# adaLN block on one core: K, Q and V's bias and the sum of phi(K) taken out of the products, through a column of ones, with smaller early loads and a new order

## The chip, the cores and the metric

The kernel runs on one core of one Trainium2 chip. The metric is the device time of one execution in microseconds (us). Engines are named as in the profile: PE (TensorE, matrix products; PEld is its weight load), DVE (VectorE), ACT (ScalarE), POOL (GpSimd) and SP (SyncE, which here only issues DMAs). PSUM is the memory into which PE writes its sums; SBUF is the working memory that all engines read.

## The reference

```python
mod = (silu(c) @ w_mod).reshape(1, 6, 1, 512)
sa, ca, ga, sb, cb, gb = (mod[:, i] for i in range(6))
h = layernorm(x) * (1 + ca) + sa                 # x: 1 x 2048 x 512
q, k, v = split(h @ wqkv)                        # 32 heads of 16
pq, pk = phi(q), phi(k)                          # phi(t) = where(t > 0, t + 1, exp(t)) + 1e-6
kv = einsum("bhsd,bhse->bhde", pk, v)
z  = einsum("bhsd->bhd", pk)
o  = einsum("bhqd,bhde->bhqe", pq, kv) / (einsum("bhqd,bhd->bhq", pq, z)[..., None] + 1e-6)
x  = x + ga * (o.reshape(1, 2048, 512) @ wo)
h  = layernorm(x) * (1 + cb) + sb
u  = gelu(h @ w_in)                              # 512 -> 1376, halves z1 and z2
g  = w_sp @ layernorm(z2) + b_sp                 # w_sp: 2048 x 2048, over the rows
x  = x + gb * ((z1 * g) @ w_out)
```

The attention is linear: with G = h^T phi(K) (512 x 512), the matrix kv follows from V's weights and G, so V itself is never formed.

## The kernel before, in words

The 2048 rows are 16 tiles of 128. Every product in full precision is made of three products of rounded halves (fp32r, "hi" and "lo"): `mm3` issues hi x hi, hi x lo and lo x hi, its lines 94, 95 and 96 in the profile. A tile's split is one copy on ACT (hi) and one subtraction on DVE or POOL (lo). A few small products are plain fp32.

Part A: load a tile of x, take mean and variance on DVE (`s1`, `ln_stats`; the power -0.5 runs on POOL), shift it (`s2`), split it (`s2_hi`, `s2_lo`: tile `hhl`), transpose it (`tx` on PE, `ht` after the split), and multiply it with K's and Q's weights (`kp`, `qp`, four chunks of 128 rows of the weights, three products of 512 columns each, so 12 products a tile). phi gives `pk` and `pq`; `g_mm` sums G over the tiles in two pairs of PSUM banks (`g0` and `g1`, alternating). From G come `gh` (its split), `kv_mm` and `kv_mask` (block diagonal), `m2_mm` (kv times wo, tile `pm`), then `den1`, `den2` and `wo_mm` (tile `po`). Part B is z (`win`), gelu, layernorm, the spatial product by seven products instead of eight (tile `P`, 2 x 2 blocks, f the sums of blocks), and the output product (tile `pn`).

Modulation: `pcol1` is the scale 1 + ca as a column of four chunks (PE products of w_mod with silu(c)), `pcol0` the shift sa. Before the change:

- `s2` makes X = mean - x, without the reciprocal deviation; `col_end` stores -(1 + ca), and `w_hi`, `w_lo` multiply K's, Q's and V's weights by it. The deviation comes later, as a scale of `phi_in` or `phi_raw`, and of `pk_hi` and `pk_lo`.
- The biases of K and Q (sa times the weights, `bias_part`, `bias_prod`, `bias_add`) are summed to rows, spread over all partitions by a product with ones (`bias_row`), kept as `kqb` and added on DVE (`phi_in`, `phi_add`).
- phi is `phi_in` or `phi_raw` from PSUM, then `phi_exp` (two ACT operations) and `phi_end` (DVE).
- V's bias is a column (`v_prod`, `v_add`, `col_v`, tile `pcolv`), which `v_bias` multiplies with z to `bz`; `kv_mask` adds it. z is the sum of phi(K) over the rows, collected tile by tile by `pk_sum`, split by `z_split` and summed over the partitions by `z_sum` (tile `pz`).

What runs when is written out by hand. A long string `ORDER` lists two-letter names of steps with their numbers (`OPS` maps them to functions; a step that is a generator goes on to its next yield at each mention). Each engine executes its instructions in the order in which the string issues them, so a waiting instruction holds up all that stand behind it on its engine. A second string, `SLOTS`, says which buffer of a pool the next tile takes: `psb` (pairs of PSUM banks), `pst` and `pso` (single banks; `pso` has two), the others in SBUF. All loads are issued by SP in the same order. `dummy` issues a product of ones with ones into a scratch tile (`warm`).

Of the kernel before, what the change touches and what calls it, by code (L numbers as in the profile page):

```python
# [37 lines left out]
u:0101100110101010
# [4 lines left out]
def block_kernel(ctx: ExitStack, tc: tile.TileContext, x, w_qkv, w_o, w_in, w_sp, b_sp, w_out,  # L43
# [64 lines left out]
    nc.gpsimd.memset(tiny, TINY)  # L108

# [19 lines left out]
    def load_w(j, h):  # L129
        load_raw(("qkv", j, h), w_qkv[j, :, 2 * h:2 * h + 2, :], parts=2 if (j, h) == (1, 0) else 1)  # L130

    def load_m(m, h):
        load_raw(("mod", m, h), w_mod[m, :, 2 * h:2 * h + 2, :], tag="zs", parts=2 if h else 1)
# [40 lines left out]
    def col_end(key):  # L174
        COL[key] = const.tile([P, KC], F32, name=f"col{key}")
        if key == 1:
            nc.scalar.activation(COL[key], CP[key][:, :, 0], AF.Copy, scale=-1.0, bias=-1.0)
# [37 lines left out]
    MEAN, RSTD = {}, {}  # L215

    def ln_stats(key, src, n):
# [10 lines left out]
        nc.gpsimd.tensor_tensor(mv[:, 1:2], ve, mhalf, op=OP.pow)  # L228

# [97 lines left out]

    def bias_row(j):
        p = ps("t", [P, D], f"bias{j}")
        for h in range(2):  # L330
            mm(p, ones, BY[j][:, h], start=h == 0, stop=h == 1)
        BY[j] = p

    def bias_end(j):
        if j == 1:
            kqb.append(sb("zs", [P, 2, D], F32, "kqb"))
        nc.scalar.activation(kqb[0][:, 1 - j], BY.pop(j), AF.Copy, bias=TINY)
# [48 lines left out]
    KP, QP, PK, PKHL, PQ, EK, TK = {}, {}, {}, {}, {}, {}, {}  # L386

    def k_mm(t, lo=0, hi=KC):
        if lo == 0:
            KP[t] = ps("o", [P, D], f"kp{t}")  # L390
        for kc in range(lo, hi):
            mm3(KP[t], HT[t][:, 0, kc], HT[t][:, 1, kc], w_of(1, kc)[:, 0], w_of(1, kc)[:, 1], kc == 0, kc == KC - 1)

    def q_mm(t):
        QP[t] = ps("o", [P, D], f"qp{t}")
        for kc in range(KC):
            mm3(QP[t], HT[t][:, 0, kc], HT[t][:, 1, kc], w_of(0, kc)[:, 0], w_of(0, kc)[:, 1], kc == 0, kc == KC - 1)
        HT.pop(t)


    def phi_in(key, p, b):
        TK[key] = sb("tb", [P, D], F32, f"t{key[0]}{key[1]}")
        nc.vector.scalar_tensor_tensor(TK[key], p, RSTD["a", key[1]], b, op0=OP.mult, op1=OP.add)


    def phi_raw(key, p):
        if key[0] == "q":
            if key[1] // 2 not in PQT:
                PQT[key[1] // 2] = sb("zs", [P, 2, D], F32, f"pq{key[1] // 2}")
            TK[key] = PQT[key[1] // 2][:, key[1] % 2, :]  # L410
        else:
            TK[key] = sb("zs", [P, D], F32, f"t{key[0]}{key[1]}")
        nc.scalar.activation(TK[key], p, AF.Copy, scale=RSTD["a", key[1]])

    def phi_add(key, b, e=0):
        ENG[e].tensor_add(TK[key], TK[key], b)

    def phi_exp(key):
        EK[key] = sb("tb", [P, D], F32, f"e{key[0]}{key[1]}")
        nc.scalar.activation(EK[key], TK[key], AF.Relu, scale=-1.0, bias=tiny)  # L420
        yield
        nc.scalar.activation(EK[key], EK[key], AF.Exp, scale=-1.0)
# [6 lines left out]
    def q_end(t):  # L429
# [820 lines left out]
```

## Time and profile before

| | us |
|---|---|
| median of 3 runs | 613.09 (611.5 to 613.3) |
| profiled execution, its own time | 614.38 |
| span of the profile | 612.6 |
| PE busy | 602.3 |
| DVE busy | 484.7 |
| ACT busy | 387.3 |
| POOL busy | 274.3 |

The span runs from the first to the last instruction; the time of an execution is the span and some 2 us around it. Busy times are sums over one engine's instructions. The mean granted clock of PE is 0.997 of full speed. In the rows of a timeline the first number is the start, the second the length, and the square brackets tell how long the engine had been idle and what ended that.

### The profile page before, as it was taken

What the parts mean: (1) busy time and instruction counts of PE and PEld (TensorE: products, weight loads), DVE (VectorE), ACT (ScalarE), POOL (GpSimd) and SP (SyncE); (2) the same over time, 40 slices, a digit from 0 to 9 for tenths busy, and PEclk for the clock granted to TensorE, in tenths of its full rate; (3) what the DMA queues carried; (4) which work ended last, traced back from release to release, by engine and by line L of the source; (5) the groups of instructions that cost most, each with busy time, mean ns of one, the idle gap of its engine ahead of it and who ended that gap; (6) DMA issues with size and microseconds to landing.
All of it is one profiled execution on the core that took longest, in us unless ns stands there. A gap on an engine that the chain in (4) does not pass through costs nothing.

```text
span 612.6 us, 9781 instructions
## 1 busy us (share of the span) xinstructions
PE 602.3 (98%) x3510; PEld 560.4 (91%) x3510; DVE 484.7 (79%) x840; ACT 387.3 (63%) x614; POOL 274.3 (45%) x249
## 2 busy tenths in 40 slices
PE   8999999999899999999999999999999999999997
PEld 8787888878788999999999999999999999998996
DVE  5889999996898976877768987755567677999874
ACT  4998999765657555955857745456464446484451
POOL 4132341414645434535652053465584524245874
PEclk9899999999999999999999999999999999999999
DMA  8555786441669564662522526275745758677673
GB/s 276 198 161 143 175 281 188 126 164 35 235 201 229 139 184 143 117 144 67 111 82 94 195 93 169 90 209 149 211 134 157 173 175 224 225 189 246 217 214 119
DMA packets 95792, 102.36 MB, mean 167 GB/s; under 512 B 65952, under 2 KB 66208, under 8 KB 95744
## 3 DMA queue, kind: packets, MB, share of 16 engines
q1 hardware_dynamic: 95744, 101.74, 57.6%
q8 instruction: 27, 0.44, 0.3%
q14 instruction: 21, 0.17, 0.1%
HBM read 61.09 MB, written 25.17 MB: 141 GB/s over the span
## 4 chain that ended last, share of the span: by engine, by line
PE 89%; DVE 4%; ACT 2%; DMA 2%; issue 1%; SPq 0%; DVEq 0%
PE P L890 34%; PE z L653 20%; PE po L96 2%; PE po L95 2%; PE pn L94 2%; PE po L94 2%; PE pn L95 2%; PE pn L96 2%; DMA raw_mod<-in_w_mod 2%; PE kp L94 2%; PE kp L96 2%; PE kp L95 2%; PE g L96 2%; PE g L94 2%; PE g L95 2%; PE qp L94 2%
## 5 line engine op out<-in xcount | busy, mean ns | idle before, releaser
L890 PE MATMUL P<-f,f 128*128 128x344 f32 x960 | 167.9, 320 | 0.0
L890 PEld LDWEIGHTS P<-f,f 128*128 128x128 f32 x960 | 154.5, 188 | 0.0
L653 PE MATMUL z<-win,ht 128*128 128x344 f32 x768 | 123.0, 320 | 0.0
L653 PEld LDWEIGHTS z<-win,ht 128*128 128x128 f32 x768 | 121.5, 188 | 1.2 <-POOL ht L270 0.3
L873 ACT ACTIVATE f<-raw_wsp 128x512 fp32r<-128x512 f32 x96 | 58.8, 628 | 62.7 <-PE P L890 29.9
L876 DVE TENSOR_TENSOR f<-raw_wsp,f 128x512 fp32r<-128x512 f32 x66 | 56.7, 878 | 21.2 <-ACT f L873 21.1
L876 POOL TENSOR_TENSOR f<-raw_wsp,f 128x512 fp32r<-128x512 f32 x30 | 42.9, 1441 | 39.2 <-ACT f L873 36.4
L228 POOL TENSOR_TENSOR mv<-ve,mhalf 128x1 f32<-128x1 f32 x48 | 33.7, 710 | 37.0 <-DVE ve L226 36.7
L890 PE MATMUL P<-bigb,f 128*128 128x344 f32 x192 | 39.3, 320 | 0.0
L890 PE MATMUL P<-biga,f 128*128 128x344 f32 x192 | 39.3, 319 | 0.0
L592 POOL TENSOR_TENSOR pq<-pq,den 128x512 f32<-128x512 f32 x16 | 18.9, 1184 | 35.0 <-DVE den L589 33.5
L94 PE MATMUL pn<-wo,ub 128*128 128x256 f32 x112 | 31.8, 284 | 1.0 <-DVE x L1080 1.0
L96 PE MATMUL pn<-wo,ub 128*128 128x256 f32 x112 | 31.7, 283 | 0.5 <-POOL ub L961 0.5
L890 PEld LDWEIGHTS P<-bigb,f 128*128 128x128 f32 x192 | 31.9, 188 | 0.0
L890 PEld LDWEIGHTS P<-biga,f 128*128 128x128 f32 x192 | 31.9, 188 | 0.0
L95 PE MATMUL pn<-wo,ub 128*128 128x256 f32 x112 | 31.7, 283 | 0.1
L238 ACT COPY ux<-us 128x1536 uint16<-128x1536 uint16 x16 | 23.5, 1470 | 8.2 <-PE P L890 7.8
L94 PE MATMUL kp<-wk,ht 128*128 128x512 f32 x64 | 26.1, 407 | 0.0
L96 PE MATMUL kp<-wk,ht 128*128 128x512 f32 x64 | 25.6, 400 | 0.0
L95 PE MATMUL kp<-wk,ht 128*128 128x512 f32 x64 | 25.5, 399 | 0.0
L94 PE MATMUL po<-m,pt 128*128 128x512 f32 x64 | 25.4, 397 | 0.0
L94 PE MATMUL qp<-wq,ht 128*128 128x512 f32 x64 | 25.3, 396 | 0.1
(268 smaller groups left out, 1491.4 us busy)
## 6 DMA issues: line engine op xcount, KB each, us to landing
raw_wsp<-in_w_sp SPq DMA_DIRECT2D x32, 512.0 KB, 4.1
wd<-wi SPq DMA_DIRECT2D x8, 688.0 KB, 4.5
win<-wd SPq DMA_DIRECT2D x8, 688.0 KB, 6.5
z1d<-z SPq DMA_DIRECT2D x16, 344.0 KB, 2.8
z1r<-z1d SPq DMA_DIRECT2D x16, 344.0 KB, 4.2
ud<-ux SPq DMA_DIRECT2D x14, 384.0 KB, 4.8
uf<-ud SPq DMA_DIRECT2D x14, 384.0 KB, 4.0
raw_mod<-in_w_mod SPq DMA_DIRECT2D x10, 512.0 KB, 5.1
```

The source lines that it names most:

```text
L94: mm(o, a_hi, b_hi, start=first, stop=False, **kw)
L95: mm(o, a_hi, b_lo, start=False, stop=False, **kw)
L96: mm(o, a_lo, b_hi, start=False, stop=last, **kw)
L228: nc.gpsimd.tensor_tensor(mv[:, 1:2], ve, mhalf, op=OP.pow)
L238: nc.scalar.copy(pl, src.bitcast(U16).rearrange("p (a b) -> p b a", b=2))
L592: nc.gpsimd.tensor_mul(q3, q3, d[:, :, None].to_broadcast([P, H, D // H]))
L653: mm(p[:, b, :HB], a[:, i, kc], win[h][:, j, kc, b * HB:(b + 1) * HB], start=kc == 0 and k == 0, stop=kc == KC - 1 and k == 2)
L873: nc.scalar.activation(SF[p, h, k][:, 0], s_src(p, h, k), AF.Copy)
L876: eng.tensor_sub(SF[p, h, k][:, 1], s_src(p, h, k), f(SF[p, h, k][:, 0]))
L890: mm(B[p, k][:, :HB], a[:, x_], b[:, y_], start=i == 1, stop=i == 3 * NP)
```

## The change

The steps of part A are rewritten, with a new `ORDER` and new `SLOTS`:

- Rows are normalised in full: `s2` computes (x - mean) times the reciprocal deviation for columns 1 to 511, on ACT (with a new small POOL operation, `nmr`, for the shift) or on DVE. Column 0 becomes 1, by a memset on POOL.
- A normalised row sums to 0, so its column 0 is minus the sum of the others. Row 0 of the weights is therefore taken off all others: W'[d] = c[d] W[d] - c[0] W[0]. For each of K, Q and V `w_row` spreads c[0] W[0] over the partitions by one plain fp32 product of 512 columns (tile `wr`, with a selector `sel` scaled by c[0]), and `w_diff` forms W' (DVE, one operation for each chunk). `w_hi` and `w_lo` split W' as before.
- Row 0 of W' takes the bias (`row_hi`, `row_lo`, from `bias_row`, now for V too), so K and Q come out of PE with their bias. With the chunk order `KO` chunk 0 comes last. Two early tiles (3 and 2) are multiplied before the bias row exists, into a pair of banks `kpe`; they get the bias on DVE (`k_bias`).
- phi is now exp on ACT straight from PSUM, and a min and max on DVE that reads the exp and the same PSUM bank again; 1e-6 is added in the split of phi(K), or by `q_tiny`.
- Row 0 of G, with ones as column 0, is the sum of phi(K): `pk_sum` and `z_split` go, and `z_sum` takes row 0 out of `gh0` with the selector. V's bias is in the products too: `v_bias` and the four `pcolv` products go, `kv_mask` is one operation for each half, and `kv_mm` issues three products of 128 columns where it issued one of 256 and one of 128.
- mod 0 is formed by four ACT products and additions (`mod_prod`, `mod_add`) instead of a chain on DVE.
- The first loads of w_mod and all of K's weights come in pieces of 256 KB.

Instructions, before and after: PE 3461 and 3478, DVE 843 and 806, ACT 617 and 582, POOL 255 and 309, SP 282 and 285.

```diff
 def load_w(j, h):
-    load_raw(("qkv", j, h), ..., parts=2 if (j, h) == (1, 0) else 1)
+    load_raw(("qkv", j, h), ..., parts=2 if j == 1 else 1)
 def load_m(m, h):
-    load_raw(("mod", m, h), ..., tag="zs", parts=2 if h else 1)
+    load_raw(("mod", m, h), ..., tag="zs", parts=2)
...
 def ln_stats(key, src, n):
     nc.gpsimd.tensor_tensor(mv[:, 1:2], ve, mhalf, op=OP.pow)
+    if key[0] == "a":
+        NMR[key[1]] = small.tile([P, 1], F32, tag="nmr", name=f"nmr{key[1]}", bufs=10)
+        nc.gpsimd.tensor_scalar(NMR[key[1]], mv[:, 0:1], mv[:, 1:2], -1.0, op0=OP.mult, op1=OP.mult)
+        nc.gpsimd.memset(src[:, 0:1], 1.0)
...
+def w_row(j):
+    WR[j] = ps("t", [P, D], f"wr{j}")
+    mm(WR[j], SEL[1], w_raw(j, 0), start=True, stop=True)
+def w_diff(j, kc):
+    o = sb("tb", [P, D], F32, f"wp{kc}") if j == 1 else w_raw(j, kc)
+    nc.vector.scalar_tensor_tensor(o, w_raw(j, kc), COL[1][:, kc:kc + 1], WR[j], op0=OP.mult, op1=OP.subtract)
 def w_hi(j, kc):
-    nc.scalar.activation(w_of(j, kc)[:, 0], w_raw(j, kc), AF.Copy, scale=COL[1][:, kc:kc + 1])
+    nc.scalar.activation(w_of(j, kc)[:, 0], WP[j, kc], AF.Copy)
...
+def row_hi(j):
+    nc.scalar.activation(w_of(j, 0)[0:1, 0], BR[j][0:1], AF.Copy)
+def row_lo(j):
+    o = w_of(j, 0)
+    nc.vector.tensor_sub(o[0:1, 1], BR[j][0:1], f(o[0:1, 0]))
...
-def s2(t):
-        nc.scalar.activation(X[t], X[t], AF.Identity, scale=-1.0, bias=MEAN["a", t])
+def s2(t, e=2):
+        x_ = X[t][:, 1:]
+        if e == 2:
+            nc.scalar.activation(x_, x_, AF.Identity, scale=RSTD["a", t], bias=NMR[t])
+        else:
+            nc.vector.tensor_scalar(x_, x_, MEAN["a", t], RSTD["a", t], op0=OP.subtract, op1=OP.mult)
...
-def phi_in(key, p, b):
-    nc.vector.scalar_tensor_tensor(TK[key], p, RSTD["a", key[1]], b, op0=OP.mult, op1=OP.add)
...
-def phi_exp(key):
-    nc.scalar.activation(EK[key], TK[key], AF.Relu, scale=-1.0, bias=tiny)
-    yield
-    nc.scalar.activation(EK[key], EK[key], AF.Exp, scale=-1.0)
-def phi_end(key, o):
-    nc.vector.scalar_tensor_tensor(o, TK.pop(key), TINY, EK.pop(key), op0=OP.max, op1=OP.add)
+def phi_exp(o, p):
+    nc.scalar.activation(o, p, AF.Exp, bias=mone)
+def phi_end(o, p):
+    nc.vector.scalar_tensor_tensor(o, o, 1.0, p, op0=OP.min, op1=OP.max)
...
+def k_bias(t):
+    o = sb("tb", [P, D], F32, f"k{t}")
+    nc.vector.tensor_add(o, KP[t], KB[0])
...
-def z_split():
-    KV["s"] = sb("s4", [P, 2, D], F32R, "pks")
-    yield from hi_lo(KV["s"][:, 0], KV["s"][:, 1], KS[0])
 def z_sum():
-        mm(KV["p"], ones, KV["s"][:, h], start=h == 0, stop=h == 1)
+        mm(KV["p"], SEL[0], GH[0][:, h], start=h == 0, stop=h == 1)
 def kv_mm(dc):
     for g in range(KC):
-        mm(p[:, g], WV[0][:, 0, dc, sl], GH[dc][:, :, sl], ...)
-        mm(p[:, g, 0], WV[0][:, 1, dc, sl], GH[dc][:, 0, sl], ...)
+        for k, (i, j) in enumerate(((0, 0), (0, 1), (1, 0))):
+            mm(p[:, g], w[:, i, dc, sl], h[:, j, sl], ...)
 def kv_mask(h):
-    nc.vector.tensor_add(m, p[:, :, 0], KV["b"][:, two])
-    nc.vector.tensor_add(m, p[:, :, 1], m)
-    nc.vector.tensor_mul(m, m, KV["mask"][:, None, :].to_broadcast([P, 2, P]))
+    nc.vector.tensor_mul(m, KV["kv"][:, two], KV["mask"][:, None, :].to_broadcast([P, 2, P]))
```

The order around the places of interest. First PE's queue from its beginning to the first K product, before; a row is line, operation, output and inputs, size, and how many follow each other (a number behind a name counts the tiles):

```order
L142 MATMUL warm_159<-ones_153 128x128 x14
L362 MATMUL tx3_227<-ident_151,x3_163 128x128 x4
L142 MATMUL warm_159<-ones_153 128x128 x9
L362 MATMUL tx2_248<-ident_151,x2_186 128x128 x4
L142 MATMUL warm_159<-ones_153 128x128 x5
L163 MATMUL pcol1_265<-sil_160,raw_mod_1_0_223 128x128 x8
L163 MATMUL pcol1_265<-sil_160,raw_mod_1_1_276 128x128 x8
L362 MATMUL tx1_300<-ident_151,x1_203 128x128 x4
L170 MATMUL pcol0_314<-ones_153,y0_258 128x1 x4
L94 MATMUL kp3_333<-wk_308,ht3_240 128x512
```

And after, up to the dummies ahead of the first K product (`kpe`, which follows):

```order
L165 MATMUL pcol1_182<-sil_162,raw_mod_1_0_168 128x128 x4
L144 MATMUL warm_161<-ones_153 128x128 x4
L165 MATMUL pcol1_182<-sil_162,raw_mod_1_0_168 128x128 x4
L165 MATMUL pcol1_182<-sil_162,raw_mod_1_1_218 128x128 x8
L395 MATMUL tx3_236<-ident_151,x3_174 128x128 x4
L144 MATMUL warm_161<-ones_153 128x128 x2
L320 MATMUL wr1_260<-raw_qkv_1_0_249,selc_233 128x512
L144 MATMUL warm_161<-ones_153 128x128 x2
L395 MATMUL tx2_297<-ident_151,x2_195 128x128 x4
L144 MATMUL warm_161<-ones_153 128x128 x10
L395 MATMUL tx0_314<-ident_151,x0_229 128x128 x4
L144 MATMUL warm_161<-ones_153 128x128 x4
```

The column products of mod 1 move from the sixth row to the very front, the 28 dummies from before everything to between the transposes (six of them behind the rows shown), the row product `wr1` is new, and the columns of mod 0 (`pcol0`) move behind the first K products.

SP's queue, from which all loads start, before:

```order
L100 DMA cT_149<-in_c 128x4
L119 DMA x3_163<-in_x 128x512
L119 DMA x0_171<-in_x 128x512
L136 DMA ident_151<-in_ident_c 128x128
L119 DMA x2_186<-in_x 128x512
L119 DMA x1_203<-in_x 128x512
L127 DMA raw_mod_1_0_223<-in_w_mod 128x1024
L127 DMA raw_mod_0_0_235<-in_w_mod 128x1024
L119 DMA x4_242<-in_x 128x512
L127 DMA raw_mod_1_1_276<-in_w_mod 128x512 x2
L127 DMA raw_mod_0_1_281<-in_w_mod 128x512 x2
L127 DMA raw_qkv_1_0_305<-in_w_qkv 128x512 x2
```

And after:

```order
L100 DMA cT_149<-in_c 128x4
L129 DMA raw_mod_1_0_168<-in_w_mod 128x512 x2
L121 DMA x3_174<-in_x 128x512
L121 DMA x2_195<-in_x 128x512
L129 DMA raw_mod_1_1_218<-in_w_mod 128x512 x2
L121 DMA x0_229<-in_x 128x512
L138 DMA ident_151<-in_ident_c 128x128
L129 DMA raw_qkv_1_0_249<-in_w_qkv 128x512 x2
L129 DMA raw_mod_0_0_267<-in_w_mod 128x512 x2
L129 DMA raw_qkv_1_1_275<-in_w_qkv 128x512 x2
L121 DMA x5_285<-in_x 128x512
L129 DMA raw_mod_0_1_293<-in_w_mod 128x512 x2
```

The four pieces of mod 1 go ahead of most tiles of x, K's weights ahead of mod 0, and what was one load of 512 KB is two of 256 KB.

PE at the place of `z_sum` (tile `pz`), before, between a tile of Q and a tile of G:

```order
L208 MATMUL pmod4_1441<-yh4_1435,ones_153 128x512
L209 MATMUL pmod4_1441<-yl4_1437,ones_153 128x512
L697 MATMUL pz_1463<-pks_1458,ones_153 128x512 x2
L94 MATMUL g0_559<-pkhl12_1429,hhl12_1323 128x512
L95 MATMUL g0_559<-pkhl12_1429,hhl12_1323 128x512
```

And after, at the end of G's last tile:

```order
L96 MATMUL g0_593<-pkhl15_1496,hhl15_1519 128x512
L94 MATMUL g1_594<-pkhl15_1496,hhl15_1519 128x512
L95 MATMUL g1_594<-pkhl15_1496,hhl15_1519 128x512
L96 MATMUL g1_594<-pkhl15_1496,hhl15_1519 128x512
L705 MATMUL pz_1549<-gh0_1546,sel_163 128x512 x2
L94 MATMUL qp11_1575<-wq1_544,ht11_1219 128x512
L95 MATMUL qp11_1575<-wq1_544,ht11_1219 128x512
```

The product that spreads the sum of phi(K) moves from the middle of G's sum to directly behind its last product, ahead of a tile of Q, since it reads `gh0`, which is split from the finished G.

More of the change, by code (lines that the diff above doesn't have):

```diff
@@ L129, in load_w @@
     def load_w(j, h):
-        load_raw(("qkv", j, h), w_qkv[j, :, 2 * h:2 * h + 2, :], parts=2 if (j, h) == (1, 0) else 1)
+        load_raw(("qkv", j, h), w_qkv[j, :, 2 * h:2 * h + 2, :], parts=2 if j == 1 else 1)
     def load_m(m, h):
-        load_raw(("mod", m, h), w_mod[m, :, 2 * h:2 * h + 2, :], tag="zs", parts=2 if h else 1)
+        load_raw(("mod", m, h), w_mod[m, :, 2 * h:2 * h + 2, :], tag="zs", parts=2)
     def load_ident():
@@ L323, in bias_split, with bias_prod, bias_add @@
+    def bias_prod(j, kc):
+        BY[j, kc] = sb("tb", [P, D], F32, f"by{j}_{kc}")
+        nc.scalar.activation(BY[j, kc], w_raw(j, kc), AF.Copy, scale=COL[0][:, kc:kc + 1],
+                             bias=1.0 / P if j < 2 and kc == 0 else 0.0)
+    def bias_add(j, kc, e=1):
+        BY[j] = BY[j, 0]
+        ENG[e].tensor_add(BY[j], BY[j], BY[j, kc])
     def bias_split(j):
@@ L326, in bias_split @@
         BY[j] = h
+    BR, KB = {}, []
     def bias_row(j):
[L329 removed]
+        BR[j] = ps("t", [P, D], f"br{j}")
         for h in range(2):
[L331 to L332 removed]
+            mm(BR[j], ones, BY[j][:, h], start=h == 0, stop=h == 1)
     def bias_end(j):
[L335 to L337 removed]
+        KB.append(sb("tb", [P, D], F32, "kb"))
+        nc.scalar.activation(KB[0], BR[j], AF.Copy)
+    def row_hi(j):
[3 more added lines that the diff above has]
+        nc.vector.tensor_sub(o[0:1, 1], BR[j][0:1], f(o[0:1, 0]))
     HHL, HT, XT = {}, {}, {}
@@ L384, in tx_lo, with kq_mm @@
         xp_lo(f"x{t}", HT[t], ENG[e])
-    KP, QP, PK, PKHL, PQ, EK, TK = {}, {}, {}, {}, {}, {}, {}
-    def k_mm(t, lo=0, hi=KC):
-        if lo == 0:
+    KP, QP, PK, PKHL, PQ = {}, {}, {}, {}, {}
+    KO = (1, 2, 3, 0)
+    def kq_mm(o, j, t, lo, hi):
+        for i in range(lo, hi):
+            kc = KO[i]
+            w = w_of(j, kc)
+            mm3(o, HT[t][:, 0, kc], HT[t][:, 1, kc], w[:, 0], w[:, 1], i == 0, i == KC - 1)
+    EARLY = (3, 2)
+    def k_mm(t, lo=0, hi=KC):
+        if lo == 0 and t in EARLY:
+            if t == EARLY[0]:
+                KP["e"] = ps("b", [P, 2, D], "kpe")
+            KP[t] = KP["e"][:, EARLY.index(t)]
+        elif lo == 0:
@@ new lines, in block_kernel @@
+        mm2 me1 me0 wr1,0 wr1,3 wl1,1 me1 wr0,2 wr1,2 q215 ws1,1 q511 d23 d22 qm9 am4 ap6 d23 lX2 at0 me0 d22 d23 q58
+        q415 d11 me2 me2 d22 ae0 ae0 at3 ae3 ae3 mm3 d18 me3 me3 q29 q49 d28 d28 am7 wo0 ah4 al4 x10 d28 ap13 ap13 d28
+        x10 x10 at2 q510 d21 d21 x10 wo3 q515 x13 x13 ah7 h20 wo4 ht0 al7,0 d21 d21 d15,0 ap8 ap8 am6,2 ah6 al6 x14 d110
+        x14 he0 x14 d111 ae2 he0 ae2 d25 x13 x13 wo7 x17 am8 z00 wr1,1 x14 d25 d25 d25 lX6 ap5 l5 h24 hp4 h23 w02 hp4
+        w12 x12 lX5 za0 zb0 am13,2 g20 ap5 x12 ah13 ah8 x12 hm4 at1 hh4 hl4 wo6 x12 h22 d114 hp3 ae1 al8 x16 x16 hp2 hp2
```

402 lines of the change are left out of this document (179 added, 223 removed).

## The prediction

> **What bounds the kernel now.** I read the page first: the busy shares, the slices, the chain.
>
> ```profile
> span 612.6 us, 9781 instructions
> ...
> PE 602.3 (98%) x3510; PEld 560.4 (91%) x3510; DVE 484.7 (79%) x840; ACT 387.3 (63%) x614; POOL 274.3 (45%) x249
> ...
> PE   8999999999899999999999999999999999999997
> ...
> PEclk9899999999999999999999999999999999999999
> ...
> PE 89%; DVE 4%; ACT 2%; DMA 2%; issue 1%; SPq 0%; DVEq 0%
> ```
>
> TensorE is busy 602.3 of 612.6 us. So a change gains time only by taking instructions from its queue, or by closing one of its few gaps. The windows by stage (start, part A to its end, the spatial products, the output) show where gaps are left:
>
> ```profile
> 0.00:22.00 22.00, 18.91 (x122) 17.44 (x123) 14.93 (x32) 13.19 (x24) 6.46 (x14) 0.92 0.82 278
> 52.00:165.00 113.00, 111.86 (x507) 91.14 (x506) 103.08 (x171) 91.10 (x146) 38.98 (x33) 1.00 0.57 169
> 335.00:547.00 212.00, 212.00 (x1348) 212.00 (x1347) 157.81 (x228) 118.01 (x193) 97.50 (x69) 1.00 0.59 169
> 547.00:612.60 65.60, 60.12 (x419) 55.47 (x418) 49.55 (x90) 27.14 (x52) 40.42 (x48) 1.00 0.62 200
> ```
>
> First number: window; then PE busy, PE weight loads, DVE, ACT, POOL, clock. In 52 to 165 DVE is busy 103 of 113 us, and still PE idles only 1.1. In 335 to 547 PE never idles. The list of waits names the gaps:
>
> ```profile
> PE tx L362 <- ACT col L177: 1.1, 1, 1.1
> PE pm L94 <- DVE m L113: 1.1, 1, 1.1
> PE pn L94 <- DVE x L1080: 1.0, 1, 1.0
> ...
> PE pcol L163 <- DMA raw_mod<-in_w_mod: 0.9, 1, 0.9
> PE pm L96 <- DVE kvh L113: 0.6, 1, 0.6
> PE pn L96 <- POOL ub L961: 0.5, 1, 0.5
> ```
>
> So the change is decided by the start, by what it adds to PE's queue, and by four waits of a microsecond or less.
>
> **The start.** PE's rows there (start, length), and the window with the reduced clock:
>
> ```profile
> 0.99 5.12 PE L142 MATMUL warm<-ones 128*128 128x128 f32 x28 [0.99 <-POOL tiny L108]
> 5.95 0.60 PE L362 MATMUL tx<-ident,x 128*128 128x128 f32 x4
> 6.39 2.17 PE L142 MATMUL warm<-ones 128*128 128x128 f32 x18
> 8.40 0.64 PE L362 MATMUL tx<-ident,x 128*128 128x128 f32 x4
> ...
> 16.85 0.96 PE L170 MATMUL pcol<-ones,y 128*128 128x1 f32 x8
> 17.67 0.48 PE L94 MATMUL kp<-wk,ht 128*128 128x512 f32 x1
> ```
> ```profile
> 18.00:22.00 4.00, 4.00 (x14) 3.22 (x14) 3.96 (x7) 4.00 (x9) 0.00 (x0) 0.57 0.59 201
> ```
>
> A plain fp32 product of 128 columns leaves two records. At first a record takes (5.95-0.99)/28 = 0.177 us, later (8.40-6.39)/18 = 0.112. A group of four transposes takes 6.39-5.95 = 0.44. In 18 to 22 the granted clock is 0.57, so 4 x 0.43 = 1.7 us are lost to it, right behind the gaps of the first 17 us.
>
> The new order begins PE's queue with the column products of mod 1, which need the first load of 256 KB. How fast such loads come:
>
> ```profile
> 1.19 0.90 SPq L119 DMA_DIRECT2D x<-in_x  x2
> ```
> ```profile
> 4.00 0.69 DVE L221 BATCH_NORM_STATS2 bst<-x 128x6 f32<-128x512 f32 x1 [4.00 <-DMA x<-in_x]
> ```
> ```profile
> 8.00:9.00 1.00, 1.00 (x12) 0.99 (x11) 0.54 (x3) 0.97 (x3) 1.00 (x2) 1.00 1.08 262
> 12.00:13.00 1.00, 0.31 (x3) 0.12 (x2) 1.00 (x1) 0.00 (x0) 1.00 (x1) 1.00 1.05 406
> ```
>
> The first piece, issued at 1.19, was used at 4.00. The last column is GB/s: 262 at 8 to 9, when w_mod came in 512 KB pieces, 406 at 12 to 13, with the first halves of w_qkv, which are 256 KB. At 406 a further piece takes 0.65 us. The first half of K's weights (its second piece is the ninth in the new order) lands at about 4.0 + 8 x 0.65 = 9.2, the second (thirteenth) at 11.8. I charge the split's three extra issues on SP nothing: 406 GB/s came with the same pieces.
>
> PE's own queue up to the first K product holds 16 column products (32 records, 3.6 us), 22 dummies (44 records, 4.9), three groups of transposes (1.3) and the row product wr1, which is plain fp32 too: four times the columns of a dummy, 4 x 0.224 = 0.9. That is 10.7; the cold records add 28 x 0.065 = 1.8. From 4.0 on this gives 16.5, later than the weights allow (wr1 stands behind some 7 us of products, at about 11), so the queue itself sets the time. Terms:
> - First K product at 16.5 instead of 17.67: -1.2.
> - The bias columns (16.85 to 17.67) and 6 dummies now stand behind it: +0.8 and 6 x 0.224 = +1.3.
> - No gap of a microsecond before the K products, so no half clock: -1.7. If the clock falls again, this comes back.
> - Waits inside the new start: DVE makes four new differences and the low parts of three tiles in a row; bounds 0 and 2.0 (the two old waits of 0.9 and 1.1), I take +0.5, because the low part of the second tile comes due within one DVE operation of the product that reads it.
>
> **PE's work behind the start.**
>
> ```profile
> 28.55 0.62 PE L331 MATMUL bias<-bh,ones 128*128 128x512 f32 x2
> 29.01 0.40 PE L94 MATMUL kp<-wk,ht 128*128 128x512 f32 x1
> ...
> 57.97 0.95 PE L170 MATMUL pcolv<-ones,vby 128*128 128x1 f32 x8
> 58.78 0.47 PE L208 MATMUL pmod<-yh,ones 128*128 128x512 f32 x1
> ```
> ```profile
> 149.19 0.28 PE L715 MATMUL pkv<-gh,wv 128*128 128x256 f32 x1
> ...
> 150.97 0.45 PE L208 MATMUL pmod<-yh,ones 128*128 128x512 f32 x1
> ```
>
> - Row products wr0 and wr2: 2 x 0.9 = +1.8. From below: two records at the 0.23 that a 512-column product of this kernel takes (28.55 to 29.01 is two), so 0.46 each.
> - A third bias row for V: +0.46. The four V columns go: 58.78-57.97, -0.81.
> - K and Q's broadcast bias and the sum of phi(K) leave DVE and POOL, not PE: nothing on the path, since DVE's 103 of 113 us hid behind PE. By the same reading the 60 additional small POOL instructions and the copies of K's early bias cost nothing, unless their result is late.
> - kv: half of it was 16 products (8 of 256, 8 of 128 columns) in 150.97-149.19 = 1.78, all 3.56. Now there are 48 of 128 columns, with as many columns in all but half as many weight loads more. From below the columns decide: 0. From above 1.78/16 = 0.111 each, 5.3 in all: +1.8. The nearest row for products bound by their weight load is pcolv: eight records of one column in 0.81, 0.101 each. 48 x 0.101 = 4.85: I take +1.3. The Trainium skill ("TensorE: Matmul & The Clock Gate", Back-to-back issue gap) gives about 81 ns for one product of 128 columns in a stream of weight load and product. By it kv would take 3.9 us, the term would be +0.3 and the whole sum -0.1, an estimate from that page; pcolv's 0.101 is this kernel's own, so it decides.
> - Moved: z_sum stood among Q and G products. It now reads gh0 and stands directly behind the last product of G.
>
> ```profile
> 143.66 0.41 PE L94 MATMUL qp<-wq,ht 128*128 128x512 f32 x1
> ```
> ```profile
> 143.86 1.08 ACT L111 ACTIVATE gh<-g 128x512 fp32r<-128x512 f32 x2 [0.53 <-PE g L96]
> ```
> ```profile
> 144.49 0.69 DVE L113 TENSOR_TENSOR gh<-g,gh 128x512 fp32r<-128x512 f32 x1 [0.43 <-ACT gh L111]
> ```
>
> Before, PE went on at 143.66 with Q while the first half of G was split, done at 144.49 + 0.69 = 145.2. The first split of after reads the bank that is finished three products (0.7) earlier, so at 144.5: PE waits 0.9, and the Q products behind z_sum with it. +0.9 (0 to 1.5).
> - The two waits of pm (1.1 on the low part of m, 0.6 on kvh): the mask is one DVE operation a half instead of three, two Q products (5.5 us) stand between kv and the first pm, and the third pm now follows the second at once instead of waiting for its split: 0 to -1.7. I take -1.7, since the 5.5 us are several times the mask and its split.
> - The two waits of pn at the end (1.0 and 0.5): the last stage computes the same in another order. 0 to -1.5, I take -0.8.
> - All other moves lie in stages in which PE has no gap to lose (212.00 of 212): 0, with a micro-wait either way in the range.
>
> Sum: -1.2+0.8+1.3-1.7+0.5+1.8+0.5-0.8+1.3+0.9-1.7-0.8 = +0.9. The profiled execution (614.38 us, span 612.6) would become 615.3; it stands 1.3 above the median, so against 613.09 I forecast **614.0 us**, which can't be told from no change (0.3%, or 1.8 us, is what a measurement of this kernel can tell).
>
> **Rivals.**
>
> Slower, by held banks. Before, one operation read a K or Q product and set its PSUM bank free. Now ACT's exp reads it and then DVE's max, and only then is it free; there are two banks.
>
> ```profile
> 146.21 0.39 PE L96 MATMUL qp<-wq,ht 128*128 128x512 f32 x1
> ```
> ```profile
> 148.10 0.74 DVE L403 SCALAR_TENSOR_TENSOR tq<-qp,mv,kqb 128x512 f32<-128x512 f32 x1
> ```
> ```profile
> 43.08 0.62 ACT L422 ACTIVATE ek<-ek 128x512 f32<-128x512 f32 x1
> ```
>
> The product that ended at 146.6 was read from 148.1, 1.5 us later. With exp and max one behind the other (0.62 + 0.74, 0.1 to hand over) the bank is free 3.0 us after its end, while the next product lasts 12 x 0.23 = 2.76: where two K or Q products stand together, the third waits 0.2. It decides from a lag of 1.3 us on. Of 30 such products 20 would give +4.0: **618.0**. For it: DVE was the busiest engine behind PE here. Against it: DVE has fewer operations now (806 for 843), and G products often stand between.
>
> Slower, by the loads: 256 KB pieces go at 262 GB/s, 1.0 us each. The thirteenth piece then lands at 16.0, difference, high and low part (0.74, 0.62, 0.69) end at 18.1, against a use about 17: with the following chunks +2.5, **616.5**. The Trainium skill ("DMA: Bandwidth & Descriptors", Bandwidth) asks for transfers of 1 MiB or more, which speaks against the split. The row at 12 to 13 speaks against that: the smaller pieces ran at 406, the larger at 262.
>
> Faster, by an order that leaves no wait: start's waits 0, z_sum's 0, kv at its columns, both pn waits gone: 0.9-0.5-0.9-1.3-0.7 = -2.5, **610.6**. For it: every one of these is an end of a bound above. Against it: z_sum stands directly behind its own source.
>
> **How the numbers follow.** The sum as it stands 0.53, of it 0.36 within 0.3%, 0.07 faster, 0.10 slower (its terms alone span about 612 to 616). Held banks 0.17, loads 0.08, both slower. No waits 0.22: 0.20 faster, 0.02 within. Together 0.27 faster, 0.38 same, 0.35 slower. The range reaches from just below the fast rival to a microsecond above the held banks: 610.0 to 619.0.
>
> **What would show it.** First K product at about 16.5 and a clock of 1.00 from 12 us on; wr rows of 0.9; kv rows 0.10 apart; one wait of z_sum (pz) on gh of about 0.9, none of pm. Waits of qp or kp on DVE's max would show the held banks; waits of pcol or wr on raw_mod or raw_qkv, the loads. Wrong I would be above all if PE's clock falls again in the new start, or if the order leaves many small waits in part A.

## The result: 617.6 us, 5.0 us slower

The changed kernel takes 617.61 us (617.0 to 618.97, 4 runs) and the kernel before 612.62 in the same comparison. The ratio is 1.0084, with a 95% interval of 1.0068 to 1.0100. The prediction was 614.0 with a range of 610.0 to 619.0: the time lies inside, but the likeliest case ("no change") did not come true, and the time lies near the 618.0 of a rival that was not its cause. That the range reaches so far is owed to this rival, so it is in part luck that the time lies inside: the sum itself fell 3.6 us short.

The profile after; its page first:

```profile
span 615.5 us, 9806 instructions
...
PE 604.4 (98%) x3526; PEld 561.4 (91%) x3526; DVE 458.5 (74%) x803; ACT 370.4 (60%) x579; POOL 303.4 (49%) x303
...
PE   6999999999999999999999999999999999999997
```

DVE lost 26 us of work and ACT 17, and nothing came of it: PE, the bound, has 2 us more. Its list of waits:

```profile
PE pcol L165 <- DMA raw_mod<-in_w_mod: 4.8, 1, 4.8
PE pn L96 <- DVE ub L961: 0.7, 1, 0.7
PE P L890 <- POOL f L876: 0.5, 1, 0.5
PE tpp L283 <- POOL pq L603: 0.4, 1, 0.4
PE po L96 <- POOL pt L276: 0.3, 1, 0.3
PE pz L705 <- DVE gh L115: 0.2, 1, 0.2
PE pn L94 <- DVE x L1080: 0.2, 1, 0.2
```

The waits of pm (1.1 and 0.6) are gone and those of pn smaller. The first product now waits 4.8 us for its load, and from there to pz, at 145 us, the list has no wait at all. In PE's timeline, the start, the bias row, z_sum and kv:

```profile
4.79 2.04 PE L165 MATMUL pcol<-sil,raw_mod 128*128 128x128 f32 x8 [4.79 <-DMA raw_mod<-in_w_mod]
6.63 1.77 PE L144 MATMUL warm<-ones 128*128 128x128 f32 x8
8.24 2.84 PE L165 MATMUL pcol<-sil,raw_mod 128*128 128x128 f32 x24
...
17.42 0.48 PE L94 MATMUL kpe<-w,ht 128*128 128x512 f32 x1
...
28.20 0.85 PE L352 MATMUL br<-bh,ones 128*128 128x512 f32 x2
...
144.58 0.49 PE L705 MATMUL pz<-gh,sel 128*128 128x512 f32 x1
145.31 0.50 PE L705 MATMUL pz<-gh,sel 128*128 128x512 f32 x1 [0.23 <-DVE gh L115]
...
151.15 4.13 PE L718 MATMUL pkv<-gh,w 128*128 128x128 f32 x36
155.12 0.45 PE L210 MATMUL pmod<-yh,ones 128*128 128x512 f32 x1
```

The two spans shown differ by 2.9 us only, the medians by 5.0. The missing 2 us are a matter of the profile of before, which the first experiment is about.

### The profile page after: what moved, and what is told of

It reads as the page before. It is cut to its first block, busy times and chain, and to the rows that moved or that the text cites. A ratio compares the mean times of both kernels' runs of the same rounds, so it can differ in the third digit from the quotient of the medians.

```text
span 615.5 us, 9806 instructions
## 1 busy us (share of the span) xinstructions
PE 604.4 (98%) x3526; PEld 561.4 (91%) x3526; DVE 458.5 (74%) x803; ACT 370.4 (60%) x579; POOL 303.4 (49%) x303
## 4 chain that ended last, share of the span: by engine, by line
PE 88%; DVE 4%; DMA 4%; ACT 2%; issue 1%; POOL 0%; SPq 0%; DVEq 0%; ACTq 0%; POOLq 0%
PE P L890 32%; PE z L664 19%; PE g L96 2%; PE g L94 2%; PE g L95 2%; PE qp L94 2%; PE qp L95 2%; PE qp L96 2%; PE po L96 2%; PE kp L94 2%; PE kp L96 2%; PE kp L95 2%; PE po L94 2%; PE po L95 2%; PE pn L96 1%; PE pn L94 1%
## 5 line engine op out<-in xcount | busy, mean ns | idle before, releaser
L876 POOL TENSOR_TENSOR f<-raw_wsp,f 128x512 fp32r<-128x512 f32 x38 | 55.2, 1463 | 60.3 <-ACT f L873 60.3
L876 DVE TENSOR_TENSOR f<-raw_wsp,f 128x512 fp32r<-128x512 f32 x58 | 46.4, 807 | 25.2 <-ACT f L873 24.7
L96 PE MATMUL po<-m,pt 128*128 128x512 f32 x64 | 25.3, 395 | 0.3 <-POOL pt L276 0.3
L94 PE MATMUL po<-m,pt 128*128 128x512 f32 x64 | 25.5, 398 | 0.0
L96 PE MATMUL g<-pkhl,hhl 128*128 128x512 f32 x64 | 25.2, 393 | 0.0
L94 PE MATMUL g<-pkhl,hhl 128*128 128x512 f32 x64 | 25.2, 393 | 0.0
```

Source lines behind the costliest of these rows:

```text
L94: mm(o, a_hi, b_hi, start=first, stop=False, **kw)
L96: mm(o, a_lo, b_hi, start=False, stop=last, **kw)
L876: eng.tensor_sub(SF[p, h, k][:, 1], s_src(p, h, k), f(SF[p, h, k][:, 0]))
```

## Experiments

Each kernel was timed against the kernel before, whose median was between 612.16 and 612.74. A difference between two changed kernels that is under about 1 us lies within what their two intervals leave. Kernels named a_ are the changed kernel with one edit, b_ the kernel before with one edit, c_ the kernel a_kv with one edit.

**b_again: the kernel before, once more.** No edit.

> The kernel before, unchanged, for a second trace of it. The two profiles differ by 2.9 us in span (612.6 and 615.5), the medians by 5.0. Clock theory: the profiled execution of before was one in which the clock fell behind the start (0.57 in 18 to 22 us, 1.7 us lost); another execution without that fall has a span near 610.8 and a clock of 1.00 there. Rival: the fall belongs to the kernel and is in every execution; a second trace shows 0.5 to 0.6 in the same place, and the 2 us are scattered elsewhere.

Measured: 612.68 us (611.66 to 614.78, 12 runs); this execution took 611.66, with a span of 609.9. The window that had the clock at 0.57, and PE's rows at the first K product and at the bias pair:

```profile
18.00:22.00 4.00, 4.00 (x19) 3.18 (x18) 3.96 (x7) 4.00 (x8) 0.08 (x1) 1.00 0.78 248
```
```profile
16.46 0.48 PE L94 MATMUL kp<-wk,ht 128*128 128x512 f32 x1
...
25.89 0.62 PE L331 MATMUL bias<-bh,ones 128*128 128x512 f32 x2
```

The clock is 1.00 there, the first K product starts at 16.46 instead of 17.67, the bias pair at 25.89 instead of 28.55. All 2.7 us between the two spans lie ahead of 26 us. So the profiled execution of before (614.38) was one of the longest of its kernel. How rare its clock fall is can be read from the mean clock of each execution: of the 66 executions of this kernel beside these experiments 12 have a mean clock of 0.997 or less, as that one has, with a median time of 614.1; the other 54 have 612.4. The clock theory is right, with nearly half of the 2.7 us in the gaps. From here on the second trace of before is the one compared with. Against it the changed kernel's trace is 5.6 us longer. Summed up from start to start over PE's instructions, by kind of product:

| part of PE's queue | us, after less before (second trace) |
|---|---|
| PE's first instruction (4.79 for 0.99) | +3.8 |
| dummies, column products, x transposes | -1.9 |
| K products and the three row products (wr) | +2.9 |
| bias rows, V's columns | -0.1 (+0.7, -0.8) |
| kv | +1.7 |
| z_sum and the end of G | +0.6 |
| pm and the transposes behind it | -1.6 |
| pn | -0.6 |
| spatial products P | +1.1 |
| the rest | -0.3 |

The other runs ask which of these are causes.

**a_kv: kv in the old form.**

```diff
-            for k, (i, j) in enumerate(((0, 0), (0, 1), (1, 0))):
-                mm(p[:, g], w[:, i, dc, sl], h[:, j, sl], ...)
+            mm(p[:, g], w[:, 0, dc, sl], h[:, :, sl], ...)
+            mm(p[:, g, 0], w[:, 1, dc, sl], h[:, 0, sl], ...)
...
-        nc.vector.tensor_mul(m, KV["kv"][:, two], mask)
+        nc.vector.tensor_copy(m, KV["kv"][:, two, 0])
+        nc.vector.tensor_add(m, KV["kv"][:, two, 1], m)
+        nc.vector.tensor_mul(m, m, mask)
```

> The changed kernel with kv_mm in the old form: 16 products of 256 and 16 of 128 columns instead of 48 of 128, and three DVE operations for each half of the mask. Queue theory (PE's own work sets the end): 5.25 - 3.57 = 1.7 us faster than the changed kernel, less up to 0.7 if the longer mask holds up the first pm product. Rival (the lost time is in waits or in the loads of the start): no change beyond 0.5 us.

Measured: 615.07 us, ratio to before 1.0041 (1.0028 to 1.0054), 2.5 less than the changed kernel. In the trace kv takes 3.58 instead of 5.25 us: 1.67, as expected. No wait appeared at pm. Another 0.75 went away among the spatial products, where the changed kernel has this gap (POOL's timeline, then PE's):

```profile
458.82 2.53 POOL L876 TENSOR_TENSOR f<-raw_wsp,f 128x512 fp32r<-128x512 f32 x2 [3.14 <-ACT f L873]
```
```profile
460.16 0.42 PE L890 MATMUL P<-bigb,f 128*128 128x344 f32 x1 [0.49 <-POOL f L876]
```

A split on POOL (1.26 each) came late by half a microsecond. In a_rows and a_zs the gap is still there, in a_kv and all kernels built on it it is not. Why it depends on kv is not shown.

The start of this execution was a later one, though nothing was changed in it:

```profile
18.17 0.48 PE L94 MATMUL kpe<-w,ht 128*128 128x512 f32 x1
...
28.84 0.84 PE L352 MATMUL br<-bh,ones 128*128 128x512 f32 x2
```

PE's first records take 0.21 us and the later ones 0.11, and how many are slow differs: 15 in the changed kernel's trace, 22 here, 28 in that of a_zs. The first K product starts at 17.42, 18.17 and 18.73. Differences of that size at the start of two traces are no effect of an edit.

**b_kv48: kv in the new form, alone, in the kernel before.**

```diff
-            mm(p[:, g], WV[0][:, 0, dc, sl], GH[dc][:, :, sl], ...)
-            mm(p[:, g, 0], WV[0][:, 1, dc, sl], GH[dc][:, 0, sl], ...)
+            for k, (i, j) in enumerate(((0, 0), (0, 1), (1, 0))):
+                mm(p[:, g, 0], WV[0][:, i, dc, sl], GH[dc][:, j, sl], ...)
...
-        nc.vector.tensor_add(m, p[:, :, 1], m)
```

> The kernel before with kv_mm alone in the new form: 48 products of 128 columns, and two DVE operations for each half of the mask instead of three. a_kv gained 2.5 us by the reverse, of which its trace gives 1.67 to kv and 0.75 to a wait among the spatial products that had nothing to do with kv. Queue theory: 1.7 us slower than before, 614.3, less up to 0.4 from the shorter mask. Rival (columns decide, or the gap at pm takes it up): no change beyond 0.5.

Measured: 615.05 us, ratio 1.0038 (1.0026 to 1.0051), 2.5 slower. Its kv in PE's timeline:

```profile
147.13 2.79 PE L716 MATMUL pkv<-gh,wv 128*128 128x128 f32 x24
149.76 0.45 PE L208 MATMUL pmod<-yh,ones 128*128 128x512 f32 x1
```

24 products in 149.76-147.13 = 2.63, 0.11 each, 48 in 5.25: kv takes 1.68 us more of PE than the old form, both ways round. The time of this kernel is no clean measure of it, though. The trace is 1.7 longer than the second one of before (span 611.6 for 609.9), but not by kv alone. Its list has one wait of pm left, and none on kvh:

```profile
PE pm L94 <- DVE m L113: 0.5, 1, 0.5
```

With the shorter mask pm and the transposes behind it take 1.4 us less, by sums of starts, so most of kv's 1.7 came back there; about as much was lost at other places (dummies and pn 0.5 each, po 0.3), and why is not shown. Besides, three of the five executions have a mean clock of 0.996 or 0.997, and in three the time stands 2.2 to 3.9 us above the span, where 1.8 is usual. So b_kv48 confirms what kv's products cost on PE, but not that 1.7 us of it reach the end in the kernel before.

**a_rows: cheap rows for Q and V.**

```diff
-        mm(WR[j], SEL[1], w_raw(j, 0), start=True, stop=True)
+        if j == 1:
+            mm(WR[j], SEL[1], w_raw(j, 0), start=True, stop=True)
+        else:
+            mm(WR[j], SEL[0], w_of(1, 0)[:, 0], start=True, stop=True)
```

> The changed kernel with the row products of Q and V (wr0, wr2) as one rounded product each, of K's first chunk instead of their own row 0 (so Q and V lack their right row difference); all else alike. Queue theory: a plain fp32 row of 512 columns takes 0.85, a rounded one 0.23, so 2 x 0.62 = 1.2 us faster. Rival (the rows stand in gaps that the start or the splits leave anyway): no change beyond 0.4 us.

Measured: 617.29 us, ratio 1.0080 (1.0066 to 1.0094), 0.3 less than the changed kernel, within what the two intervals leave. In the traces, by starts of single products: K's first product 0.28 later, the first bias row 0.16 later, the first G product again 0.28 later, the last 0.37 earlier. So the row of V (behind the first G products) brought its 0.65, and the row of Q, ahead of the bias row, at most 0.1 of its 0.62. Up to the bias row something else stands close behind PE's queue, so that a lighter queue gains next to nothing. That is neither theory whole: the queue theory holds behind the start, the rival ahead of it.

**c_front: ten dummies ahead of the first load.**

```diff
-        se si lm1,0 si lx3 s13 cr1,0 du1 du2 du3 du4 s13 ...
+        du1 du2 du3 du4 du5 du6 du7 du8 du9 du10 se si lm1,0 si lx3 s13 cr1,0 s13 ...
```

> a_kv with 10 of the 28 dummies at the very front of PE's queue, where it waits 4.8 us for its first load anyway. Queue theory: the queue behind the load gets 10 x 0.224 = 2.2 us shorter and its 16 slow records (0.2 each) run at the full clock, 1.6 more: first K product near 13.6, the whole 3 to 4 us faster, 611 to 612. Data theory (the first K product's low weights come from POOL at 16.4, and the bias row from a chain on ACT and DVE that ends at 28): first K product near 16, bias row still at about 28, less than 1 us faster, 614.2 to 615.0.

Measured: 614.56 us, ratio 1.0033 (1.0020 to 1.0046), 0.5 less than a_kv.

```profile
0.97 4.14 PE L144 MATMUL warm<-ones 128*128 128x128 f32 x20 [0.97 <-POOL ones L104]
...
8.30 2.05 PE L165 MATMUL pcol<-sil,raw_mod 128*128 128x128 f32 x16 [1.12 <-DMA raw_mod<-in_w_mod]
...
17.36 0.47 PE L94 MATMUL kpe<-w,ht 128*128 128x512 f32 x1
...
28.13 0.86 PE L352 MATMUL br<-bh,ones 128*128 128x512 f32 x2
```

PE's queue is 3.8 us lighter behind the load than in a_kv, and the first K product starts only 0.8 earlier than there (17.36 for 18.17), the bias row 0.7 (28.13 for 28.84); against the changed kernel's trace, with its earlier start, it is 0.1 (17.42 and 28.20). The rest went into new waits. The queue theory is out as a forecast of what a lighter start gains (13.6 and 3 to 4 us); the data theory gave 614.2 to 615.0.

**c_none: no dummies behind these ten at all.** c_front with du11 to du28 taken out of the order.

> c_front (614.56 us) without its other 18 dummies: PE's queue up to the bias row is another 15 x 0.224 = 3.4 us shorter, 18 x 0.224 = 4.0 in all. Queue theory: 3 to 4 us faster, 610.5 to 611.5. Data theory (the bias row of K waits for the chain from mod 0's loads over its column, four products on ACT, three additions and a split): bias row still at about 28, PE waits in the dummies' place, within 0.7 us of c_front; if the waits let the clock fall, up to 2 us slower.

Measured: 614.94 us, ratio 1.0045 (1.0031 to 1.0058), the same as c_front. PE's rows with a wait, then the window 12 to 18 of it and of c_front:

```profile
8.75 2.05 PE L165 MATMUL pcol<-sil,raw_mod 128*128 128x128 f32 x16 [1.47 <-DMA raw_mod<-in_w_mod]
...
15.96 1.09 PE L395 MATMUL tx<-ident,x 128*128 128x128 f32 x4 [2.15 <-ACT w L328]
28.35 0.50 PE L352 MATMUL br<-bh,ones 128*128 128x512 f32 x1 [0.36 <-DVE bh L115]
```
```profile
12.00:18.00 6.00, 3.29 (x13) 2.29 (x12) 5.74 (x13) 4.95 (x9) 5.33 (x7) 0.79 1.03 370
```
```profile
12.00:18.00 6.00, 5.07 (x37) 4.12 (x36) 5.74 (x12) 4.77 (x10) 5.47 (x7) 1.00 1.03 388
```

Without dummies PE is busy 3.29 us of the 6 instead of 5.07, waits 2.15 for ACT at the transposes of a tile, and its clock falls to 0.79; the first five K products start some 0.43 apart instead of 0.23, which takes 1.0 of what was saved. The second product of the bias row still starts only at 28.35, when the low part of the bias is there. 4.0 us of PE work are gone and the time is the same: in this kernel the data set the time up to 28 us, not PE's queue.

In the changed kernel it is the queue: there the chain that ended last, followed back from its end, runs from 4.79 to the bias row over PE alone, and here it comes to 28.35 over a load of x, DVE, ACT and POOL. The two stand so close that lightening one only brings out the other. The chain of the data is seen on ACT and DVE of this kernel:

```profile
21.56 0.17 ACT L178 ACTIVATE col<-pcol 128x4 f32<-128x4 f32 x1 [0.41 <-PE pcol L172]
21.77 3.79 ACT L335 ACTIVATE by<-raw_qkv,col 128x512 f32<-128x512 f32 x6
...
26.68 0.63 ACT L113 ACTIVATE bh<-by 128x512 fp32r<-128x512 f32 x1 [0.64 <-DVE by L340]
```
```profile
24.37 2.28 DVE L340 TENSOR_TENSOR by<-by,by 128x512 f32<-128x512 f32 x3
...
27.62 0.68 DVE L115 TENSOR_TENSOR bh<-by,bh 128x512 fp32r<-128x512 f32 x1
```

From the column of mod 0 at 21.6: six products on ACT (four are K's), three additions on DVE, the split on both, 6.7 us in a row. Before the change the bias row had no product waiting for it, since K got its bias afterwards on DVE. Now it is a row of K's weights, and the last chunk of every K tile that is not one of the two early ones needs it.

**c_du: without the six dummies among the K products.** a_kv with du23 to du28 taken out.

> a_kv without the six dummies that stand among the K products. Queue theory: 6 x 0.224 = 1.3 us faster, 613.8. Data theory: three of them stand ahead of the bias row, where PE waits for data, and bring nothing; the three behind it bring 0.7: 614.4. If the clock needs them, it falls below 1.00 there and the time rises.

Measured: 615.48 us, ratio 1.0051 (1.0035 to 1.0068), 0.4 above a_kv and not below. Two of its waits:

```profile
PE br L352 <- DVE bh L115: 0.5, 1, 0.5
...
PE kp L94 <- DVE pk L449: 0.2, 1, 0.2
```

The bias row waits for its split, and one K product for its bank (DVE's max). This execution had a late start, with the first K product at 18.92 instead of a_kv's 18.17, so the spans can't be compared; from that product to the 49th it is 16.1 us for 16.4. So these dummies cost at most 0.3 of the 1.3 that the queue theory charged: most of what they leave free turns into waits, behind the bias row too, which is less than the data theory said. The clock stayed at 1.00.

**c_loads: the old sizes of the loads.**

```diff
-        load_raw(("qkv", j, h), ..., parts=2 if j == 1 else 1)
+        load_raw(("qkv", j, h), ..., parts=2 if (j, h) == (1, 0) else 1)
-        load_raw(("mod", m, h), ..., tag="zs", parts=2)
+        load_raw(("mod", m, h), ..., tag="zs", parts=2 if h else 1)
```

> a_kv with the pieces of the loads as in the kernel before (first halves of both modulations and K's second half as one load of 512 KB), the order kept. Theory (first use sets the start): PE's first product has to wait for 512 KB instead of 256, about 1.2 us more, 615.5 to 616.3. Rival (small pieces are slow, the second rival on the loads): 1 to 3 us faster, 612 to 614.

Measured: 615.83 us, ratio 1.0062 (1.0043 to 1.0082), 0.8 above a_kv. In its list of waits:

```profile
PE pcol L165 <- DMA raw_mod<-in_w_mod: 6.1, 1, 6.1
```

PE's first product is 1.1 us later than with 256 KB (6.05 for 4.98). How much of it reaches the end is not clear: the two traces differ by 0.1 us in span, and the intervals of the two kernels overlap. But nothing came faster, so the small pieces are not slow.

**b_loads: the new sizes of the loads alone, in the kernel before.** The reverse edit.

> The kernel before with the loads alone changed: all early loads of w_mod and K's weights in pieces of 256 KB, order kept. Theory from c_loads (what counts is when the first piece that PE waits for lands): dummies and transposes cover PE until 10 us, so at most the wait of pcol on raw_mod in some executions goes, 0 to 0.9 us faster, 611.8 to 612.7. Rival (small pieces are slow): 0.5 to 2 us slower.

Measured: 612.43 us, ratio 0.9995 (0.9986 to 1.0003). No difference; the rival is out here too.

**a_zs: z_sum behind a tile of Q.**

```diff
-        gh0 gh0 zs gh2 zr d17,0 d27 gh3 lX0 gh3 wy1 wy2 d14 d24 d16 gh1 qm11 d24 gh1 wr0,0
+        gh0 gh0 gh2 gh3 lX0 gh3 wy1 wy2 gh1 gh1 qm11 zs zr d17,0 d27 d14 d24 d16 d24 wr0,0
```

> The changed kernel with z_sum behind the next tile of Q instead of directly behind G's last product, and all four splits of G ahead of the first den steps. Queue theory: the wait of pz on gh0 goes, 0.6 us faster (0.16 ahead of its first half, 0.4 ahead of its second). Rival: den and the split of kv come later by the tile of Q (2.8 us), and the wait turns up again at pm or at the first po: no change.

Measured: 626.06 us, ratio 1.0217 (1.0201 to 1.0233), 8.5 slower than the changed kernel. Both theories missed by far. PE's rows, and its window 155 to 160:

```profile
148.01 0.62 PE L705 MATMUL pz<-gh,sel 128*128 128x512 f32 x2
155.12 0.79 PE L94 MATMUL qp<-wq,ht 128*128 128x512 f32 x1 [6.49 <-DVE pq L449]
155.72 0.63 PE L95 MATMUL qp<-wq,ht 128*128 128x512 f32 x1
156.14 0.63 PE L96 MATMUL qp<-wq,ht 128*128 128x512 f32 x1
```
```profile
155.00:160.00 5.00, 4.88 (x12) 3.81 (x13) 1.92 (x5) 1.58 (x3) 4.80 (x5) 0.50 0.27 52
```

pz now waits for nothing. But pz and the Q tile had changed places in the two banks of `pso`, so the next Q tile takes the bank of the Q tile just made, whose max stands on DVE behind the den steps, which wait for z. That is the mechanism of the held banks, here at 6.5 us. Behind it the clock is 0.50 and the next 12 products start 0.43 apart instead of 0.23: 2.5 us more.

**c_zs: the same with a bank of another pool for pz.** a_kv with the order of a_zs, `KV["p"] = ps("t", ...)` instead of `ps("o", ...)`, and the letters of `pst` and `pso` in SLOTS moved accordingly.

> a_kv (615.07 us, 2.3 above before) with z_sum behind the next tile of Q, as in a_zs, but with a PSUM bank of its own pool for pz (pst instead of pso), so that the next Q tiles no longer take a bank that waits for the den chain. Bank theory of a_zs (its 8 us came from qp waiting for the bank that DVE's max had not yet read, since DVE stood at den waiting for z): the 6.5 us wait of qp on pq is gone, and the 0.6 us wait of pz too: 614.5. Rival (the later z itself holds up den, and with it the transposes of phi(Q)): waits at tpp or po, 616 or more.

Measured: 616.38 us, ratio 1.0071 (1.0053 to 1.0090), 1.3 slower than a_kv. From its list of waits:

```profile
PE pm L96 <- DVE kvh L115: 1.4, 2, 0.7
...
PE pkv L717 <- DVE gh L115: 0.5, 1, 0.5
```

qp's wait is gone, as the bank theory said, and pz's 0.6 too. But kv now waits 0.5 for a split of G, and pm 1.4 for that of kv: the work around z_sum has no room. The rival was right in the result, at other places than it named.

**b_best: three operations moved on DVE, in the kernel before.**

```diff
-        qm8 q18 kx0 ap6 wr0,3 qm15 kx0 mm1 mm0
+        qm8 kx0 kx0 q18 ap6 wr0,3 qm15 mm1 mm0
...
-        me0 me0 kx1 kx1 d23 d23 d23 al4 ah7 at0 ae0 wr0,2 lX0 d22 d22 lX4 me1 mm3
+        me0 me0 me1 kx1 kx1 d23 d23 d23 al4 ah7 at0 ae0 wr0,2 lX0 d22 d22 lX4 mm3
...
-        Uo4 Uc3,1 Om0,6 Oa1,1 Ua0,3 Oa0,4
+        Uo4 Om0,6 Oa1,1 Ua0,3 Oa0,4 Uc3,1
```

> The kernel before with three operations earlier or later on DVE, and nothing else: the low part of kvh's first half ahead of a phi of Q, the low part of m's second product ahead of kvh's second half, and one sum of the output stage behind two additions to x. What the changed kernel's order gained at pm and pn (1.55 and 0.64 by the traces), without its new work. Theory: the waits of pm (1.1 and 0.6) and part of that of pn (1.0) go, 1.6 to 2.4 us faster, 610.2 to 611.1. Rival (each wait hides another right behind it, as with z_sum): less than 0.6 faster.

Measured: 610.17 us (609.34 to 611.22, 5 runs), ratio 0.9962 (0.9948 to 0.9975), 2.4 faster than the kernel before: the fastest version here. What is left of the waits in question:

```profile
PE pn L96 <- POOL ub L961: 0.4, 1, 0.4
PE pm L94 <- DVE m L113: 0.2, 1, 0.2
```

1.1 became 0.2, and the 0.6 on kvh and the 1.0 on x are gone. By sums of starts pm and the transposes behind it take 1.5 us less and pn 1.0, no less in all than what the changed kernel gained there (1.6 and 0.6); 0.4 came back at po.

## Why the prediction came out as it did

Its frame was right: PE's queue sets the end, relief of DVE and ACT brings nothing, and the sum is of small terms. The sum came out 3.6 us too low, mainly by two steps: the start, and the way from the profiled execution to the median. Step by step:

- **First K product (-1.2).** 17.42 instead of 16.5. The first load of w_mod was used at 4.79, not at 4.00 like the first load of x before, and that is most of the miss; from the load on PE's queue took 12.6 us, where the step had summed 12.5 (the slow first records cost 1.65, for 1.8). So "the queue itself sets the time" holds for the changed kernel's trace. What the step did not see is how close the data stand behind the queue: c_front and c_none took 3.8 and another 4.0 us out of it, for 0.5 us and nothing. The walk had followed the weights, and not mod 0's bias down to the row that K's last chunk now needs. Its reading that 256 KB pieces run at 406 GB/s because they are small is not borne out either: from 8 to 9 us c_loads, with pieces of 512 KB, moved 389 GB/s, and b_loads, with 256 KB, 246.
- **No half clock (-1.7).** The changed kernel has a clock of 1.00 there, but so have the second trace of the kernel before and, by their mean clocks, 54 of its 66 executions. Against the slow profiled execution the gain is real; against the median there is none. The prediction saw that this execution stood 1.3 above the median, counted the gain in full, and then took the 1.3 off once more, from 615.3 to 614.0. This is the largest single error of the sum. Against the second trace the first K product is not 1.2 earlier but 1.0 later. That the gaps of a microsecond bring the fall is not shown either: b_best has gaps of 0.5 and 1.1 in the same place and a clock of 1.00 from 18 to 22.
- **Bias columns and dummies (+2.1), waits in the new start (+0.5).** From the first K product to the first bias row the two kernels need 10.8 and 9.4 us, to the 49th K product 16.5 and 13.0. PE's rows in the changed kernel's trace split the 3.5 us between them: 0.9 for the columns of mod 0, 0.9 for the six dummies, 0.9 for Q's row product, 0.5 more for the same 48 K products, 0.4 at the bias row and the transposes, and less than 0.1 of it is idle. The sum had 0.8, 1.3, 0.9 and, as waits, 0.5 for this: 3.5 as well. The dummies fill time in which PE would wait (c_du, c_none); taking them out brings little.
- **Rows (+1.8).** 0.9 each, as taken. a_rows won back the 0.65 of V's; of Q's 0.62 it was at most 0.1, because the data stand close behind it.
- **kv (+1.3).** +1.7, by PE's rows in a_kv and b_kv48: 0.111 us a product, the upper end of the term's bounds. The rate of 0.101 from pcolv was the wrong row to be near to. By the 81 ns of the Trainium skill ("TensorE: Matmul & The Clock Gate", Back-to-back issue gap) the 48 products would have taken 3.9 us, an estimate from that page; the traces show 5.25, so here the measurement decides against it.
- **z_sum (+0.9).** +0.6: PE waited less for gh0 than taken. That it wasn't won back by a later place (a_zs, c_zs) was not foreseen.
- **pm (-1.7) and pn (-0.8).** -1.6 and -0.6: right, and b_best has the same gain without the rest of the change.
- **Moves in the other stages (0).** The spatial products have +1.1, of it 0.75 that went away in a_kv together with the wait for a late split on POOL. A stage in which PE had no gap to lose could still gain one.

Of the rivals, the held banks did not come true in the changed kernel: its list has no wait of kp or qp on pk or pq. The mechanism is real, as a_zs (6.5 us) and c_du (0.2) show. The slow loads are refuted by c_loads and b_loads: larger pieces made the changed kernel no faster, and smaller ones the kernel before no slower. The Trainium skill ("DMA: Bandwidth & Descriptors", Bandwidth) asks for 1 MiB or more; no run here has loads of that size; but between 256 and 512 KB the larger size gained nothing, and PE got its first operand 1.1 us later. The rival of an order without waits failed at z_sum, where its counter-argument stood, and at kv.

What stays open is what a shorter chain of the bias would gain: no kernel was run with one, nor with one and a lighter queue together. So the 3.5 us up to the 49th K product are read from PE's rows, and no run wins them back.

## What to carry to other kernels

Take a second trace of the kernel before, or at least hold each term of the sum against the difference between the profiled execution and the median: a gap that only one long execution has is no gain for anyone, and the difference may be taken off once, not twice. Folding a bias into the products takes work off engines with spare time and ties the products to the chain that makes the bias; follow that chain from its load to its first reader too, since PE's queue and the chain can stand so close that lightening one gains nothing. Where PE is busy 98% of the time, look for the few waits whose operands stand behind other work on DVE, and move those operations: 2.4 us here, against 5.0 lost by a rewrite.

## What the runs showed of the hardware

- Two executions of one program differ by 2.7 us in the first 28: in the first trace gaps of 0.9 and 1.1 us and then a clock of 0.57 over 4 us, in the second no such fall. 12 of 66 executions have a mean clock of 0.997 or less, as the first has, and their median time is 1.6 us longer. Gaps of 0.5 and 1.1 in b_best came without a fall.
- PE's first records in the changed start take 0.21 us instead of 0.11, and how many do differs between executions: 15, 22 and 28 in the traces of the changed kernel, a_kv and a_zs.
- After one wait of 6.5 us the granted clock was 0.50 for 5 us; the 2.15 us wait of c_none came with 0.79 in its window of 6 us.
- A product of 128 columns takes 0.111 us in a row of 48, so that three take 0.33, where a product of 256 and one of 128, with as many columns and one weight load fewer, take 0.22 together.
- The first load of 256 KB, issued at the same time, was used at 4.00 us as rows of x and at 4.79 as a part of w_mod.
